# Start of a two-stage kernel: the first angle table, the first transform and the first weights in another order

## Chip, core and metric

The kernel runs on one core of one Trainium2 chip. The metric is the device time of one execution in microseconds, smaller is better. A core has five engines that run their own instruction queues in order: TensorE (PE, matrix products), VectorE (DVE), ScalarE (ACT), GpSimd (POOL) and SyncE (SP). They wait for each other through semaphores. PSUM is where TensorE writes, SBUF is the memory of the core.

## The reference

`x` has 8 batches of 3008 rows by 256 columns. The first stage is the real part of a two-dimensional Fourier transform of each batch, the second a feed-forward layer with a squared ReLU on every row:

```python
def _attn_ref(x) -> np.ndarray:
    X = np.fft.fft(x, axis=1)
    X = np.fft.fft(X, axis=2)
    return X.real.astype(np.float32)

def _moe_ref(x, w_in, w_out) -> np.ndarray:
    h = np.maximum(x @ w_in, 0.0)
    return (h * h @ w_out).astype(np.float32)
```

`w_in` is 256 by 2048, `w_out` 2048 by 256. The result has 24064 rows of 256 columns.

## The kernel before

The rows of a batch are folded first: sums and differences of row n and row S-n, and of column d and column D-d, so that the transform over the rows needs only a part of the products. A folded batch has two units: `(i, 0)` with the odd frequencies and `(i, 1)` with the even ones. For each unit TensorE multiplies folded rows by tables of cosines and sines (`z_steps`, L560; the matmul is L581), and ACT and VectorE bring the result into windows of up to 512 columns, `zc` and `zs` (L586, L592, L599, L610). The transform over the 256 columns is not made for each row: it is multiplied into `w_in` beforehand. `gh_step` (L519) multiplies a block of 512 columns of `w_in` by the cosines `c_all` and the sines `s_n` of the column transform, VectorE scales the result into `gh` (`gh_scale`, L513, here L517), and `gh_turn` (L532) makes a third copy with the sign turned.

The windows then run one after the other: `gh` times `zc` and `zs` (L859, L860, L868, L877, L882; L938 and L944 in the first window), ReLU on ACT (L891, L950) or VectorE (L889), square on VectorE or ACT, and the product with `w_out` (L704) for the window before, whose rows go out through SP. Folds and transforms of later batches are spread over the steps of the windows. The order on every engine is the order in which the program writes the instructions; no scheduler changes it.

All that the change touches is written ahead of the first window:

- POOL issues the loads of the first `x` (a direct transfer of the first two quarters, then one gathered transfer for the third and one for the fourth, L127 and L132), with small index tables in between, then the two halves of `w_in` (L180). Later it issues the load of `w_out` (L329).
- `table_steps(0)` (L207) makes the table for unit 0: 128 partitions, 6 rows, 376 frequencies. Rows stand in the order `RQ = (1, 3, 5, 0, 2, 4)`; set 0 is rows 1, 3, 5, set 1 is rows 0, 2, 4. `freq` (L220) makes the frequencies `kf` on VectorE from `irow`, a cast of the integers `irow_i`. `args` (L227) makes three rows of rounded turns on ACT, `turns` (L236) turns them into multiples of the length on VectorE or POOL. The angle, `kf` times the row number plus that multiple, is made in one of two ways: by `mods` (L250), a multiply-add on VectorE for each row, or by `kns` (L240), the products on ACT, and `sums` (L246), one addition over three rows on VectorE. Before, set 0 goes by `mods` and set 1 by `kns` and `sums`.
- `sins` (L259) takes the sine of three rows on ACT. `weigh` (L273) multiplies row 1 of the sines by a weight `wgt`, on POOL. A cosine row is the mirrored sine row 6-r, so `coss` (L262) is a matmul with a mirroring matrix `perm` (made on POOL, L326) and an eviction on ACT (L271), two rows at a time: rows 1 and 3, rows 5 and 0, rows 2 and 4.
- `c_all` and `s_n` are made from 129 columns of `irow` on VectorE (L289 to L301) and by two sines on ACT (L315, L317), with one column of `s_n` copied from `c_all` (L331).
- `fold_steps(0)` (L372) folds the first batch: `u_half` (L395) subtracts the first two quarters and copies one row of `x`, `u_odd` (L399) subtracts the other two, `u_part(sg)` (L402) makes `cs` and folds the columns into `od[:, sg]`, `edge` (L406) copies one column of it on ACT, `nyq` (L450) fills another by two small matmuls and a VectorE copy (L455), `v_even` (L409) makes the other half of the fold and issues the load of the next batch.
- `idle(n)` (L304) puts n matmuls on TensorE whose result nobody reads.
- `z0(part, h)` is the first transform: part 0 with cosines, part 1 with sines, h is the set. After h 0 ACT copies the sum out of PSUM (`es`), and the second half adds to the same PSUM tile.

PSUM tiles come from three pools: `ps_h` (2 tiles of two banks), `ps_o` (2 tiles of one bank, tag `po`) and `ps_z` (2). A new tile of a pool waits until the one two before it has been read.

The order of the start before, from L309 on:

```python
    run(f0s["u_half"], f0s["u_odd"], lambda: f0s["u_part"](0))
    to["coss"](0)
    idle(4)
    to["coss"](1)
    to["coss"](2)
    idle(5)
    f0s["edge"]()
    run(*z0(0, 0))
    gh_pg = gh_step(0)
    run(lambda: f0s["u_part"](1), f0s["nyq"])
    gh_scale(gh[:, 0:2, 0:512], gh_pg, False)
    run(*z0(0, 1))
    run(*z0(1, 0))
    gh_turn(0)
    gh_step(1, False)
```

Of the kernel before, what the change touches and what calls it, by code (L numbers as in the profile page):

```python
# [29 lines left out]
def kernel(  # L30
# [152 lines left out]
    def small(shape, name):  # L183
        return const.tile(shape, F32, name=name)
# [7 lines left out]
    nraw = small([P, R], "nraw")  # L192
    nc.vector.tensor_copy(nraw, nvec_i)
    irow = small([P, NE], "irow")
    nc.vector.tensor_copy(irow, irow_i)
# [11 lines left out]
    def table_steps(e):  # L207
# [12 lines left out]
        def freq():  # L220
            kf = st["kf"] = tmp.tile([P, NE], F32, name="kf", tag="kf")[:, 0:n]
            i = 0
            for k0, kstep, cnt in unit_runs[e][0]:
                nc.vector.tensor_scalar(out=kf[:, i : i + cnt], in0=irow[:, i : i + cnt], scalar1=float(kstep), scalar2=float(k0 - kstep * i), op0=ALU.mult, op1=ALU.add)
                i += cnt

        def args(h):  # L227
# [19 lines left out]
            m = st["m", h][:, 0:nr, 0:n]  # L247
            nc.vector.tensor_tensor(m, m, st["t", h][:, 0:nr, 0:n], op=ALU.add)

        def mods(h):  # L250
            m = st["m", h] = tmp.tile([P, 3, NE], F32, name="m", tag="tm")
            for j in range(nr):
                r = row(h, j)
                nc.vector.scalar_tensor_tensor(out=m[:, j, 0:n], in0=st["kf"], scalar=vec[:, r : r + 1], in1=st["t", h][:, j, 0:n], op0=ALU.mult, op1=ALU.add)

        def absm(h):
            nc.vector.tensor_scalar(out=st["t", h][:, 0:nr, 0:n].bitcast(I32), in0=st["m", h][:, 0:nr, 0:n].bitcast(I32), scalar1=0x7FFFFFFF, scalar2=None, op0=ALU.bitwise_and)

        def sins(h):  # L259
            nc.scalar.activation(sin_t[:, 3 * h : 3 * h + nr, :], st["m", h][:, 0:nr, 0:n], AF.Sin, bias=0.0, scale=wk)  # L260

        def coss(h):  # L262
            if e:
                nc.scalar.activation(cos_t, st["t", h][:, 0:nr, 0:n], AF.Sin, bias=halfpi[:, 0:1], scale=-wk)
                return

            pc = ps_h.tile([P, 2, 512], F32, name="pc", tag="psh")
            for j in range(2):
                r = RQ[2 * h + j]
                nc.tensor.matmul(pc[:, j, 0:n], perm[1 if r else 0], sin_t[:, RQ.index(6 - r if r else 0), :], start=True, stop=True)  # L270
            nc.scalar.activation(cos_t[:, 2 * h : 2 * h + 2, :], pc[:, :, 0:n], AF.Copy, bias=0.0, scale=1.0)  # L271

        def weigh():  # L273
            if e:
                for t in (cos_t, sin_t):
                    for r in range(2):
                        nc.vector.tensor_scalar(out=t[:, r, :], in0=t[:, r, :], scalar1=wge[:, r : r + 1], scalar2=None, op0=ALU.mult)
                return

            q = RQ.index(1)  # L280
            nc.gpsimd.tensor_scalar(out=sin_t[:, q, :], in0=sin_t[:, q, :], scalar1=wgt[:, 0:1], scalar2=1.0, op0=ALU.mult, op1=ALU.mult)
# [22 lines left out]
    def idle(n):  # L304

        for i in range(n):
            nc.tensor.matmul(pw[:, 0 : 3 * P], spn[:, 0, 0, :], spn.rearrange("p c r d -> p (c r d)")[:, 0 : 3 * P], start=True, stop=True)
# [7 lines left out]
    nc.scalar.activation(s_n, am, AF.Sin, bias=0.0, scale=-wd)  # L315
    c_all = const.tile([P, 2, P + 1], F16, name="c_all")
    nc.scalar.activation(c_all, at, AF.Sin, bias=halfpi[:, 0:1], scale=-wd)  # L317
# [6 lines left out]
    perm = [const.tile([P, P], F16, name=f"perm{i}") for i in range(2)]  # L324
    for i in (1, 0):
        nc.gpsimd.tensor_scalar(out=perm[i], in0=prow_i, scalar1=float(P - 1 - i), scalar2=None, op0=ALU.is_equal)  # L326
    to["sums"](1)

    nc.gpsimd.dma_start(out=wout16, in_=moe_w_out.rearrange("(c p) o -> p c o", p=P))  # L329
# [3 lines left out]
    pick = const.tile([P, 1], F16, name="pick")  # L333
    nc.gpsimd.memset(pick, 0.0)
# [4 lines left out]
    evec_i = iota([P, 2], [[1, 2]], 0, 2, "evec_i")
    idx["c"] = iota([P, 1], [[1, 1]], P - 1, -1, "idx_c")  # L340
    nc.gpsimd.memset(idx["c"][0:2, :], P - 3)
    idx["f"] = iota([P, 1], [[1, 1]], -1, 1, "idx_f")
    nc.gpsimd.memset(idx["f"][0:1, :], 0)
    evec = small([P, 2], "evec")
    nc.gpsimd.tensor_copy(evec, evec_i)
    evs = small([P, 2], "evs")
    nc.gpsimd.tensor_scalar(out=evs, in0=evec, scalar1=1.0 / S, scalar2=None, op0=ALU.mult)
    wge = small([P, 2], "wge")
    wg2 = small([P, 2], "wg2")
    nc.gpsimd.tensor_scalar(out=wge, in0=evec, scalar1=float(G), scalar2=0.5, op0=ALU.is_le, op1=ALU.mult)  # L350
    nc.gpsimd.tensor_scalar(out=wg2, in0=evec, scalar1=float(G), scalar2=0.5, op0=ALU.is_lt, op1=ALU.mult)
    nc.gpsimd.tensor_tensor(wge, wge, wg2, op=ALU.add)
    nc.gpsimd.tensor_scalar(out=wg2, in0=evec, scalar1=0.0, scalar2=-0.5, op0=ALU.is_equal, op1=ALU.mult)
    nc.gpsimd.tensor_tensor(wge, wge, wg2, op=ALU.add)
    to["sins"](1)
    folded = {}

    fe = fo = None
# [13 lines left out]
    def fold_steps(i):  # L372
# [21 lines left out]

        def u_half():  # L395
            nc.vector.tensor_tensor(u[:, 0], t[:, 0], t[:, 1], op=ALU.subtract)
            nc.vector.tensor_copy(t[0:1, 2, 0, :], t[0:1, 0, R - 1, :])

        def u_odd():  # L399
# [109 lines left out]
        return {"edge": edge, "u_half": u_half, "u_odd": u_odd, "u_part": u_part, "v_even": v_even, "v_part": v_part, "d_even": d_even, "n_cos": n_cos, "odds": odds, "d_odd": d_odd, "load": load, "n_sin": n_sin, "nyq": nyq, "even": even, "away": away, "back": back, "late": late}  # L509

    gh = const.tile([P, 3, F], F16, name="gh")

    def gh_scale(out, pg, act):  # L513
        if act:
            nc.scalar.activation(out, pg, AF.Copy, bias=0.0, scale=-1.0 / HS)
        else:
            nc.vector.tensor_scalar(out=out, in0=pg, scalar1=-1.0 / HS, scalar2=None, op0=ALU.mult)  # L517

    def gh_step(cc, act=None):  # L519

        f0 = cc * 512
        fw = f0 % (F // 2)
        pg = ps_h.tile([P, 2, 512], F32, name="pg", tag="psh") if act is None else None
        for i, t in enumerate((c_all, s_n)):
            pt = ps_o.tile([P, 512], F32, name="pg", tag="po") if pg is None else pg[:, i, :]
            for c in range(2):
                nc.tensor.matmul(pt, t[:, c, 0:P], w16[f0 // (F // 2)][:, c, fw : fw + 512], start=(c == 0), stop=(c == 1))
# [535 lines left out]
```

## Time and profile before

| | |
|---|---|
| median of three runs | 598.36 us (597.36 to 598.58) |
| the profiled execution | 597.31 us |
| its span, first to last instruction | 595.5 us |
| mean granted TensorE clock | 0.999 |
| instructions | 11299 |

The profile is one execution. Busy time is given for PE, PEld (TensorE's weight loads, which overlap PE), DVE, ACT and POOL. A row of the timeline is one instruction, or several of a line merged: its start, its length, engine, line, operation, what it writes and reads, and in brackets how long the engine stood idle before it and what ended that. The chain is followed back from the last instruction to what released each step.

### The profile page before, as it was taken

What the parts mean: (1) busy time and instruction counts of PE and PEld (TensorE: products, weight loads), DVE (VectorE), ACT (ScalarE), POOL (GpSimd) and SP (SyncE); (2) the same over time, 40 slices, a digit from 0 to 9 for tenths busy, and PEclk for the clock granted to TensorE, in tenths of its full rate; (3) what the DMA queues carried; (4) which work ended last, traced back from release to release, by engine and by line L of the source; (5) the groups of instructions that cost most, each with busy time, mean ns of one, the idle gap of its engine ahead of it and who ended that gap; (6) DMA issues with size and microseconds to landing.
All of it is one profiled execution on the core that took longest, in us unless ns stands there. A gap on an engine that the chain in (4) does not pass through costs nothing.

```text
span 595.5 us, 11299 instructions
## 1 busy us (share of the span) xinstructions
PE 584.9 (98%) x4421; PEld 424.9 (71%) x4421; DVE 497.0 (83%) x582; ACT 462.2 (78%) x617; POOL 243.9 (41%) x304
## 2 busy tenths in 40 slices
PE   7999999999999999999999999999999999999997
PEld 4567786776776777777777777777777777777786
DVE  8988686987989778979899799979899799888871
ACT  6796777967797787788878788877877788788762
POOL 8411423166514506183253651446505724425310
PEclk9999999999999999999999999999999999999999
DMA  8946421137211461246123442145312321211212
GB/s 149 154 87 149 123 73 44 48 108 148 61 44 55 129 138 49 72 101 155 41 59 108 94 116 58 38 121 115 90 39 90 87 58 37 61 47 48 61 56 70
DMA packets 37624, 50.33 MB, mean 85 GB/s; under 512 B 4589, under 2 KB 30755, under 8 KB 37571
## 3 DMA queue, kind: packets, MB, share of 16 engines
q0 software_dynamic: 10400, 24.94, 20.6%
q1 hardware_dynamic: 26899, 24.44, 13.6%
q8 instruction: 34, 0.56, 0.4%
q10 hardware_dynamic: 272, 0.23, 0.1%
q14 instruction: 19, 0.16, 0.1%
HBM read 36.42 MB, written 27.86 MB: 108 GB/s over the span
## 4 chain that ended last, share of the span: by engine, by line
PE 81%; DVE 10%; ACT 3%; POOL 2%; issue 2%; DMA 1%; DVEq 0%; ACTq 0%; POOLq 0%
PE po L704 47%; PE ph L882 6%; PE ph L859 6%; PE ph L860 6%; PE ph L877 6%; PE ph L868 5%; PE pz L581 4%; DVE h L898 2%; DVE t L872 2%; DVE h L889 2%; DMA xo<-in_x_dram,idx_r 1%; ACT h L891 1%; DVE zc L610 1%; ACT h L902 1%; POOL xo L132 1%
## 5 line engine op out<-in xcount | busy, mean ns | idle before, releaser
L704 PE MATMUL po<-wout,h 128*128 128x256 f16 (+1 forms) x3024 | 364.8, 273 | 0.0
L704 PEld LDWEIGHTS <-h 128*128 128x128 f16 (+1 forms) x3024 | 296.8, 98 | 75.1
L891 ACT ACTIVATE h<-ph 128x1024 f16<-128x1024 f32 (+3 forms) x301 | 287.6, 991 | 64.2 <-PE ph L877 41.1
L898 DVE TENSOR_TENSOR h<-h 128x2048 f16<-128x2048 f16 (+7 forms) x199 | 189.9, 960 | 22.1 <-ACT h L891 18.9
L818 POOL TENSOR_SCALAR n<-zn,g2n 128x512 f32<-128x512 f16 (+3 forms) x166 | 156.2, 954 | 68.7 <-DMA zn<-rd 55.5
L872 DVE SCALAR_TENSOR_TENSOR t<-ph,n 128x1024 f32<-128x1024 f32 (+3 forms) x83 | 99.1, 1194 | 37.5 <-PE ph L868 32.1
L889 DVE CUSTOM_DVE_ANT_0 h<-t,ph 128x1024 f16<-128x1024 f32 x74 | 90.0, 1216 | 15.5 <-ACT h L891 15.1
L902 ACT ACTIVATE h<-h 128x1024 f16<-128x1024 f16 (+3 forms) x87 | 90.3, 1038 | 0.5
L719 ACT ACTIVATE osb<-po 128x512 f32<-128x512 f32 (+3 forms) x95 | 55.0, 584 | 37.0 <-PE po L704 32.5
L859 PE MATMUL ph<-zc,gh 128*128 128x512 f16 (+3 forms) x218 | 80.3, 369 | 0.4 <-ACT h L950 0.3
L860 PE MATMUL ph<-zs,gh 128*128 128x512 f16 (+3 forms) x218 | 80.2, 368 | 0.0
L810 POOL DMA_DIRECT2D zn<-rd x22 | 12.7, 579 | 161.9 <-DMA rd<-zs 153.6
L882 PE MATMUL ph<-zs,gh 128*128 128x512 f16 (+3 forms) x218 | 62.5, 368 | 0.3 <-ACT h L891 0.3
L877 PE MATMUL ph<-zs,gh 128*128 128x512 f16 (+3 forms) x166 | 48.4, 373 | 0.9 <-DVE t L872 0.4
L868 PE MATMUL ph<-zc,gh 128*128 128x512 f16 (+3 forms) x166 | 48.4, 373 | 0.0
L859 PEld LDWEIGHTS <-gh 128*128 128x128 f16 x218 | 21.2, 97 | 22.9 <-DVE h L889 1.6
L860 PEld LDWEIGHTS <-gh 128*128 128x128 f16 x218 | 21.3, 98 | 22.1 <-issue 0.9
L868 PEld LDWEIGHTS <-gh 128*128 128x128 f16 x166 | 16.2, 98 | 18.9 <-issue 0.5
L882 PEld LDWEIGHTS <-gh 128*128 128x128 f16 x218 | 20.2, 98 | 4.1 <-issue 0.7
L586 ACT ACTIVATE es<-pz 128x376 f32<-128x376 f32 (+1 forms) x32 | 14.8, 485 | 8.9 <-PE pz L581 8.7
L464 POOL DMA_DIRECT2D scr<-ev x8 | 4.7, 582 | 40.7 <-DVE ev L460 34.8
L132 POOL DMA_INDIRECT xo<-in_x_dram,idx_r x15 | 17.7, 1182 | 4.5 <-issue 4.3
(143 smaller groups left out, 368.2 us busy)
## 6 DMA issues: line engine op xcount, KB each, us to landing
out_dram<-osb SPq DMA_DIRECT2D x77, 128.0 KB
xo<-in_x_dram POOLq DMA_DIRECT2D x7, 768.0 KB, 6.8
scr<-ev POOLq DMA_DIRECT2D x8, 390.0 KB, 4.0
zn<-rd POOLq DMA_DIRECT2D x19, 128.0 KB, 3.9
rb<-scr POOLq DMA_DIRECT2D x16, 130.0 KB, 3.9
out_dram<-osb SPq DMA_DIRECT2D x12, 94.0 KB
w<-in_moe_w_in_dram POOLq DMA_DIRECT2D x2, 512.0 KB, 10.0
wout<-in_moe_w_out_dram POOLq DMA_DIRECT2D x1, 1024.0 KB, 11.0
```

The costliest lines, as they stand in the source:

```text
L704: nc.tensor.matmul(po[0:m, j * D : (j + 1) * D], h2[:, fc, q : q + m], wout16[:, fc, :], start=(fc == 0 and not both), stop=(fc == NFC - 1 ...
L818: nc.gpsimd.tensor_scalar(out=n2[:, a, 0:wn1], in0=zns[wt][:, 0:wn1], scalar1=g2n[:, fc : fc + 1], scalar2=1.0, op0=ALU.mult, op1=ALU.mult)
L859: nc.tensor.matmul(ph[:, a, 0:wn], gh[:, 0, f0 : f0 + P], zcw[:, 0:wn], start=True, stop=False)
L860: nc.tensor.matmul(ph[:, a, 0:wn], gh[:, 1, f0 : f0 + P], zsw[:, 0:wn], start=False, stop=True)
L868: nc.tensor.matmul(ph[:, a, 0:wn], gh[:, 0, f0 : f0 + P], zcw[:, 0:wn], start=True, stop=True)
L872: nc.vector.scalar_tensor_tensor(out=t2[:, :, 0:wn], in0=phs[s][:, :, 0:wn], scalar=-2.0, in1=n2s[w, s][:, :, 0:wn], op0=ALU.mult, op1=ALU ...
L877: nc.tensor.matmul(phs[s][:, a, 0:wn], gh[:, 1, f0 : f0 + P], zsw[:, 0:wn], start=False, stop=True, skip_group_check=True)
L882: nc.tensor.matmul(phs[s][:, a, 0:wn], gh[:, 2, f0 : f0 + P], zsw[:, 0:wn], start=False, stop=True, skip_group_check=True)
L889: nc.vector._custom_dve(TENSOR_ADD_SAT, out=h, in0=t2s[s][:, :, 0:wn], in1=phs[s][:, :, 0:wn], s0=BIG, s1=0.0)
L891: nc.scalar.activation(h, phs[s][:, :, 0:wn], AF.Relu, bias=0.0, scale=-1.0)
L898: nc.vector.tensor_tensor(h, h, h, op=ALU.mult)
L902: nc.scalar.activation(h, h, AF.Square, bias=0.0, scale=1.0)
```

## The change

`freq` of set `table_steps(0)` reads the integers `irow_i` directly, and the cast to `irow` moves behind it. Set 0 of the angles is made by `kns` and `sums`, set 1 by `mods` in two calls, two rows and one row. The sines of set 1 are taken in two calls as well. `weigh` moves from POOL to ACT, and the two instructions for `wgt` from POOL to VectorE. `coss` has four parts instead of three (rows 1 and 3, row 5, row 0, rows 2 and 4), its matmuls and its eviction can be written apart, and its one-row parts take their PSUM tile from `ps_o`. The row copy of `u_half` becomes a step of its own, `u_row`. `s_n` and `c_all` come after the first three cosine rows on ACT. Fillers are 48 and 14 instead of 44, 4 and 5. The small POOL setup from `pick` to `wge` comes after the second set of sines, the `w_out` load directly after the second `perm`. In the first transform the last three cosine rows come after `gh_step(0)`, and `gh_step(1)`, `gh_turn(0)`, `z0(1, 0)` come ahead of `z0(0, 1)`. The functions of `fold_steps` to `z_steps` are defined earlier in the file, otherwise unchanged.

```diff
     irow = small([P, NE], "irow")
-    nc.vector.tensor_copy(irow, irow_i)
...
-                nc.vector.tensor_scalar(out=kf[:, i : i + cnt], in0=irow[:, i : i + cnt], scalar1=float(kstep), scalar2=float(k0 - kstep * i), op0=ALU.mult, op1=ALU.add)
+                nc.vector.tensor_scalar(out=kf[:, i : i + cnt], in0=(irow if e else irow_i)[:, i : i + cnt], scalar1=float(kstep), scalar2=float(k0 - kstep * i), op0=ALU.mult, op1=ALU.add)
...
-        def mods(h):
-            m = st["m", h] = tmp.tile([P, 3, NE], F32, name="m", tag="tm")
-            for j in range(nr):
+        def mods(h, js=None):
+            if not js or 0 in js:
+                st["m", h] = tmp.tile([P, 3, NE], F32, name="m", tag="tm")
+            m = st["m", h]
+            for j in js or range(nr):
...
-        def sins(h):
-            nc.scalar.activation(sin_t[:, 3 * h : 3 * h + nr, :], st["m", h][:, 0:nr, 0:n], AF.Sin, bias=0.0, scale=wk)
+        def sins(h, a=0, z=nr):
+            nc.scalar.activation(sin_t[:, 3 * h + a : 3 * h + z, :], st["m", h][:, a:z, 0:n], AF.Sin, bias=0.0, scale=wk)
...
-            pc = ps_h.tile([P, 2, 512], F32, name="pc", tag="psh")
-            for j in range(2):
-                r = RQ[2 * h + j]
+            q0, nq = ((0, 2), (2, 1), (3, 1), (4, 2))[h]
+            pc = ps_h.tile([P, 2, 512], F32, name="pc", tag="psh") if nq > 1 else ps_o.tile([P, 512], F32, name="pc", tag="po").rearrange("p (j n) -> p j n", j=1)
+            for j in range(nq):
+                r = RQ[q0 + j]
...
-            nc.scalar.activation(cos_t[:, 2 * h : 2 * h + 2, :], pc[:, :, 0:n], AF.Copy, bias=0.0, scale=1.0)
+            return lambda: nc.scalar.activation(cos_t[:, q0 : q0 + nq, :], pc[:, :, 0:n], AF.Copy, bias=0.0, scale=1.0)
...
-            nc.gpsimd.tensor_scalar(out=sin_t[:, q, :], in0=sin_t[:, q, :], scalar1=wgt[:, 0:1], scalar2=1.0, op0=ALU.mult, op1=ALU.mult)
+            nc.scalar.activation(sin_t[:, q, :], sin_t[:, q, :], AF.Copy, bias=0.0, scale=wgt)
...
     to["freq"]()
+    nc.vector.tensor_copy(irow, irow_i)
...
-    idle(44)
-    to["args"](0)
-    to["args"](1)
-    to["kns"](1)
-    nc.scalar.activation(s_n, am, AF.Sin, bias=0.0, scale=-wd)
-    nc.scalar.activation(c_all, at, AF.Sin, bias=halfpi[:, 0:1], scale=-wd)
-    to["turns"](0)
-    to["mods"](0)
-    to["turns"](1, nc.gpsimd)
-    nc.gpsimd.tensor_scalar(out=wgt, in0=nraw[:, 1:2], scalar1=float(Q), scalar2=-0.5, op0=ALU.is_equal, op1=ALU.mult)
-    nc.gpsimd.tensor_scalar(out=wgt, in0=wgt, scalar1=1.0, scalar2=None, op0=ALU.add)
-    for i in (1, 0):
-        nc.gpsimd.tensor_scalar(out=perm[i], in0=prow_i, scalar1=float(P - 1 - i), scalar2=None, op0=ALU.is_equal)
-    to["sums"](1)
-    nc.gpsimd.dma_start(out=wout16, in_=moe_w_out.rearrange("(c p) o -> p c o", p=P))
-    to["sins"](0)
-    nc.scalar.activation(s_n[:, :, 0:1], c_all[:, :, P : P + 1], AF.Copy, bias=0.0, scale=0.5)
-    to["weigh"]()
...
-    to["sins"](1)
...
-    run(f0s["u_half"], f0s["u_odd"], lambda: f0s["u_part"](0))
-    to["coss"](0)
-    idle(4)
-    to["coss"](1)
-    to["coss"](2)
-    idle(5)
+    def make_perm(i):
+        nc.gpsimd.tensor_scalar(out=perm[i], in0=prow_i, scalar1=float(P - 1 - i), scalar2=None, op0=ALU.is_equal)
+
+    idle(48)
+    to["args"](0)
+    to["kns"](0)
+    to["args"](1)
+    make_perm(1)
+    to["turns"](0)
+    to["sums"](0)
+    to["turns"](1, nc.gpsimd)
+    make_perm(0)
+    nc.gpsimd.dma_start(out=wout16, in_=moe_w_out.rearrange("(c p) o -> p c o", p=P))
+    to["sins"](0)
+    nc.vector.tensor_scalar(out=wgt, in0=nraw[:, 1:2], scalar1=float(Q), scalar2=-0.5, op0=ALU.is_equal, op1=ALU.mult)
+    nc.vector.tensor_scalar(out=wgt, in0=wgt, scalar1=1.0, scalar2=None, op0=ALU.add)
+    to["weigh"]()
+    f0s["u_half"]()
+    to["mods"](1, (0, 1))
+    run(f0s["u_row"], f0s["u_odd"], lambda: f0s["u_part"](0))
+    to["mods"](1, (2,))
+    for c in (to["coss"](0), to["coss"](1)):
+        c()
+    idle(14)
+    nc.scalar.activation(s_n, am, AF.Sin, bias=0.0, scale=-wd)
+    nc.scalar.activation(c_all, at, AF.Sin, bias=halfpi[:, 0:1], scale=-wd)
+    nc.scalar.activation(s_n[:, :, 0:1], c_all[:, :, P : P + 1], AF.Copy, bias=0.0, scale=0.5)
+    to["sins"](1, 0, 2)
     f0s["edge"]()
+    to["sins"](1, 2, 3)
...
     run(*z0(0, 0))
     gh_pg = gh_step(0)
+    for c in (to["coss"](2), to["coss"](3)):
+        c()
     run(lambda: f0s["u_part"](1), f0s["nyq"])
     gh_scale(gh[:, 0:2, 0:512], gh_pg, False)
-    run(*z0(0, 1))
-    run(*z0(1, 0))
-    gh_turn(0)
-    gh_step(1, False)
+    gh_step(1, False)
+    gh_turn(0)
+    run(*z0(1, 0))
+    run(*z0(0, 1))
     rm = z0(0, 2) + z0(1, 2)
```

More of the change, by code (lines that the diff above doesn't have):

```diff
@@ L307, in idle @@
             nc.tensor.matmul(pw[:, 0 : 3 * P], spn[:, 0, 0, :], spn.rearrange("p c r d -> p (c r d)")[:, 0 : 3 * P], start=True, stop=True)
-    idle(44)
-    to["args"](0)
-    to["args"](1)
-    to["kns"](1)
+    perm = [const.tile([P, P], F16, name=f"perm{i}") for i in range(2)]
     wd = 2.0 * math.pi / D
     s_n = const.tile([P, 2, P + 1], F16, name="s_n")
-    nc.scalar.activation(s_n, am, AF.Sin, bias=0.0, scale=-wd)
     c_all = const.tile([P, 2, P + 1], F16, name="c_all")
-    nc.scalar.activation(c_all, at, AF.Sin, bias=halfpi[:, 0:1], scale=-wd)
@@ L339 @@
[L339 to L354, printed above, removed]
-    to["sins"](1)
     folded = {}
@@ L396, in u_half, with u_row @@
             nc.vector.tensor_tensor(u[:, 0], t[:, 0], t[:, 1], op=ALU.subtract)
+        def u_row():
             nc.vector.tensor_copy(t[0:1, 2, 0, :], t[0:1, 0, R - 1, :])
@@ L508, in fold_steps @@
         late = [lambda: fold8(0), lambda: fold8(1), lambda: fold16(0), lambda: fold16(1), nyq8]
-        return {"edge": edge, "u_half": u_half, "u_odd": u_odd, "u_part": u_part, "v_even": v_even, "v_part": v_part, "d_even": d_even, "n_cos": n_cos, "odds": odds, "d_odd": d_odd, "load": load, "n_sin": n_sin, "nyq": nyq, "even": even, "away": away, "back": back, "late": late}
+        return {"u_row": u_row, "edge": edge, "u_half": u_half, "u_odd": u_odd, "u_part": u_part, "v_even": v_even, "v_part": v_part, "d_even": d_even, "n_cos": n_cos, "odds": odds, "d_odd": d_odd, "load": load, "n_sin": n_sin, "nyq": nyq, "even": even, "away": away, "back": back, "late": late}
     gh = const.tile([P, 3, F], F16, name="gh")
@@ new lines @@
+    for c in (to["coss"](0), to["coss"](1)):
[5 more added lines that the diff above has]
+    to["sins"](1, 0, 2)
+    f0s["edge"]()
+    to["sins"](1, 2, 3)
+    pick = const.tile([P, 1], F16, name="pick")
+    nc.gpsimd.memset(pick, 0.0)
+    nc.gpsimd.memset(pick[0:1, :], -2.0)
@@ new lines @@
+    turn2 = small([P, 1], "turn2")
+    nc.gpsimd.tensor_scalar(out=turn2, in0=dvec[:, 0:1], scalar1=0.0, scalar2=2.0, op0=ALU.is_equal, op1=ALU.mult)
+    nc.gpsimd.tensor_scalar(out=turn2, in0=turn2, scalar1=-2.0, scalar2=None, op0=ALU.add)
+    evec_i = iota([P, 2], [[1, 2]], 0, 2, "evec_i")
+    idx["c"] = iota([P, 1], [[1, 1]], P - 1, -1, "idx_c")
+    nc.gpsimd.memset(idx["c"][0:2, :], P - 3)
+    idx["f"] = iota([P, 1], [[1, 1]], -1, 1, "idx_f")
+    nc.gpsimd.memset(idx["f"][0:1, :], 0)
@@ new lines @@
+    evec = small([P, 2], "evec")
+    nc.gpsimd.tensor_copy(evec, evec_i)
+    evs = small([P, 2], "evs")
+    nc.gpsimd.tensor_scalar(out=evs, in0=evec, scalar1=1.0 / S, scalar2=None, op0=ALU.mult)
+    wge = small([P, 2], "wge")
+    wg2 = small([P, 2], "wg2")
+    nc.gpsimd.tensor_scalar(out=wge, in0=evec, scalar1=float(G), scalar2=0.5, op0=ALU.is_le, op1=ALU.mult)
+    nc.gpsimd.tensor_scalar(out=wg2, in0=evec, scalar1=float(G), scalar2=0.5, op0=ALU.is_lt, op1=ALU.mult)
+    nc.gpsimd.tensor_tensor(wge, wge, wg2, op=ALU.add)
@@ L653 @@
+    nc.gpsimd.tensor_scalar(out=wg2, in0=evec, scalar1=0.0, scalar2=-0.5, op0=ALU.is_equal, op1=ALU.mult)
+    nc.gpsimd.tensor_tensor(wge, wge, wg2, op=ALU.add)
     run(*z0(0, 0))
     gh_pg = gh_step(0)
+    for c in (to["coss"](2), to["coss"](3)):
+        c()
     run(lambda: f0s["u_part"](1), f0s["nyq"])
     gh_scale(gh[:, 0:2, 0:512], gh_pg, False)
+    gh_step(1, False)
+    gh_turn(0)
+    run(*z0(1, 0))
     run(*z0(0, 1))
-    run(*z0(1, 0))
-    gh_turn(0)
-    gh_step(1, False)
     rm = z0(0, 2) + z0(1, 2)
```

7 lines of the change are left out of this document (removed).

## The prediction

> **What bounds the kernel now.** I read the page's busy times and its chain first, then the timeline of the first 50 us engine by engine, since the change ends there. Columns of the timeline: start and length in us, engine, line, operation, and in brackets the idle time before it with what ended it.
>
> ```profile
> PE 584.9 (98%) x4421; PEld 424.9 (71%) x4421; DVE 497.0 (83%) x582; ACT 462.2 (78%) x617; POOL 243.9 (41%) x304
> PE 81%; DVE 10%; ACT 3%; POOL 2%; issue 2%; DMA 1%; DVEq 0%; ACTq 0%; POOLq 0%
> ```
>
> TensorE is busy nearly throughout and is 81% of the chain, so work saved on another engine is worth only what it brings TensorE's queue forward. TensorE's opening:
>
> ```profile
> 1.22 10.05 PE L307 MATMUL pw<-spn 128*128 128x384 f16 x44 [1.22 <-DVE spn L189]
> 6.63 4.24 PEld L307 LDWEIGHTS <-spn 128*128 128x128 f16 x26 [0.17 <-issue]
> 14.44 0.80 PE L270 MATMUL pc<-sin,perm 128*128 128x376 f16 x4 [2.00 <-POOL pick L334]
> 16.62 0.65 PE L581 MATMUL pz<-cos,od 128*128 128x376 f16 x3 [0.56 <-ACT od L407]
> 18.98 0.59 PE L527 MATMUL pg<-w,c_all 128*128 128x512 f16 x2
> 19.84 0.64 PE L581 MATMUL pz<-sin,od 128*128 128x376 f16 x3
> 20.94 0.57 PE L938 MATMUL ph<-zs,gh 128*128 128x240 f16 x4
> 23.86 0.59 PE L527 MATMUL pg<-w,c_all 128*128 128x512 f16 x2
> 24.46 0.59 PE L527 MATMUL pg<-w,s_n 128*128 128x512 f16 x2
> 44.10 0.65 PE L581 MATMUL pz<-sin,od 128*128 128x376 f16 x3 [0.46 <-DVE od L455]
> ```
>
> The first 44 matmuls are filler. The first useful transform, z0(0,0), starts at 16.62, held by ACT's edge copy (L407). Before it TensorE stood still for 2.00 us: the view names the POOL instruction after it, but the matmul's wait is on `weigh` (L281), which ends at 14.39 below. ACT:
>
> ```profile
> 4.04 3.10 ACT L232 ACTIVATE t<-kf,nvs 128x376 f32<-128x376 f32 x6 [1.81 <-DVE kf L224]
> 7.05 1.59 ACT L244 ACTIVATE m<-kf,nvec 128x376 f32<-128x376 f32 x3
> 8.54 0.40 ACT L315 ACTIVATE s_n<-am 128x258 f16<-128x258 f32 x1
> 8.85 0.50 ACT L317 ACTIVATE c_all<-at,halfpi 128x258 f16<-128x258 f32 x1
> 10.12 1.14 ACT L260 ACTIVATE sin<-m 128x1128 f16<-128x1128 f32 x1 [0.77 <-DVE m L254]
> 14.96 1.49 ACT L271 ACTIVATE cos<-pc 128x752 f16<-128x752 f32 x2 [1.74 <-PE pc L270]
> 16.33 0.23 ACT L407 ACTIVATE od<-cs 128x6 f16<-128x6 f16 x1
> 17.31 0.48 ACT L586 ACTIVATE es<-pz 128x376 f32<-128x376 f32 x1 [0.74 <-PE pz L581]
> ```
>
> **First angles: args, kns, turns, sums.** VectorE and POOL:
>
> ```profile
> 2.91 0.36 DVE L195 CAST irow<-irow_i 128x377 f32<-128x377 int32 x1
> 3.66 0.35 DVE L224 TENSOR_SCALAR kf<-irow 128x376 f32<-128x376 f32 x1
> 6.32 1.07 DVE L238 TENSOR_SCALAR t<-t 128x1128 f32<-128x1128 f32 x1
> 9.94 1.41 DVE L248 TENSOR_TENSOR m<-m,t 128x1128 f32<-128x1128 f32 x1
> ...
> 7.44 1.14 POOL L238 TENSOR_SCALAR t<-t 128x1128 f32<-128x1128 f32 x1
> 9.66 2.09 POOL L326 TENSOR_SCALAR perm<-prow_i 128x128 f16<-128x128 int32 x2
> 11.71 1.23 POOL L329 DMA_DIRECT2D wout<-in_moe_w_out_dram  x1
> 13.03 1.36 POOL L281 TENSOR_SCALAR sin<-sin,wgt 128x376 f16<-128x376 f16 x1
> ```
>
> The cast of irow leaves the path to kf: kf can come at most 0.36 earlier; I take 0.25 (ACT starts at 3.80), as the casts overlap their neighbours. Nine ACT instructions go from 4.04 to 8.54, 0.50 each. With the order args(0), kns(0), args(1), kns(0) is done at 6.9 and args(1) at 8.4. turns(0) still ends at 7.39, because the am/at work before it on VectorE keeps its length (the cast only moves behind kf). Then sums(0), at its own 1.41, runs 7.45 to 8.87, where the three L254 ran until 10.02. So sins(0) runs 8.97 to 10.11 instead of 10.12 to 11.26: 1.15 us earlier. `weigh` on ACT is one more 376-column instruction: between 0.48 (L586) and 0.60 (L232); with 0.60 it ends at 10.75 instead of 14.39 on POOL.
>
> **Filler and cosines.** 48 fillers instead of 44: 26 weight loads take 4.24 us, 0.16 each, so four more cost 0.65 and TensorE reaches the first cosine matmuls at 11.75, not when the sines are ready. This eats 1 us of the gain above, and it is cover too: a delay of the sines up to 1 us costs nothing. Three matmuls 0.16 apart, the first two done at 12.23; from there ACT's queue sets the path: cosines of rows 1 and 3 at 12.27 (0.70 start to start, half of 1.49 rounded down for overlap), row 5 (0.39, half the columns), s_n (0.31, from 8.54 to 8.85), c_all and its one-column fix (0.63), sins(1) of two rows (0.74, two thirds of 1.14), edge (0.23). Sum 3.00: edge ends at 15.27 and z0(0,0) can start at 15.32, against 16.62: 1.30 us earlier, if VectorE's od is there.
>
> **VectorE around u.**
>
> ```profile
> L254 DVE SCALAR_TENSOR_TENSOR m<-kf,nvec,t x3: 598/600/1551, 7.4 to 9.4; 128x376 f32<-128x376 f32 x3
> 11.28 1.04 DVE L396 TENSOR_TENSOR u<-xo 128x1536 f16<-128x1536 f16 x1
> 12.24 0.71 DVE L397 COPY xo<-xo 1x256 f16<-1x256 f16 x1
> 12.99 0.96 DVE L400 TENSOR_TENSOR u<-xo 128x1536 f16<-128x1536 f16 x1
> 13.98 1.22 DVE L403 TENSOR_TENSOR cs<-u 128x1536 f16<-128x1536 f16 x1
> 15.23 0.57 DVE L370 TENSOR_TENSOR od<-cs 128x768 f16<-128x768 f16 x1
> 18.20 0.18 DVE L455 CAST od<-py 128x6 f16<-128x6 f32 x1 [0.95 <-PE py L454]
> 21.46 1.75 DVE L410 TENSOR_TENSOR v<-xo 128x3072 f16<-128x3072 f16 x1
> ...
> L400 DVEq EVENT_SEMAPHORE  x1: 21/21/21, 12.1 to 12.1; - x1
> ```
>
> The last row is u_odd's wait for the last quarter of x, over at 12.1: u_odd can't start sooner, so at most 0.9 of its 12.99 is to be had. Two things may keep it later. One L254 took 1551 ns instead of 600 beside POOL's turns(1) (7.44 to 8.58), and L397 ended at 12.95 just as POOL's issue of wout ended at 12.94: VectorE waits out long POOL instructions. Now turns(1) starts on POOL when args(1) or sums(0) ends, so it runs to between 9.6 and 10.0, and u_half stands behind it to between 10.4 and 11.0. Two mods of 0.52 follow, and the row copy waits out the wout issue again, which ends between 11.7 and 12.6 as one perm goes ahead of turns(1). Bounds of u_odd: 12.1 and 12.95; I take 12.5. cs at 13.5 costs 0.96 like L400, not 1.22, because `weigh` no longer runs on POOL beside it. od is done at 15.05, inside ACT's 15.32 (15.5 at the late bound). The third mods (0.60), cs and od of the other part end at 17.07, against 17.26.
>
> A rule on the same rows: the Trainium skill, SBUF — State Buffer, section Who interferes with whom, says that a VectorE instruction with two SBUF inputs and a GpSimd one that reads SBUF exclude each other for the whole instruction, whichever starts first. The 1551 ns agree; the two perms beside L248 agree less: it took 1.41 for 1128 columns, where three undisturbed L254 take 1.57 for as many. What the rule in full would make of the time is the slow rival below.
>
> **TensorE from z0(0,0).** From 16.62 to 20.94 it took 4.32 before. Moved in between are the three late cosine matmuls: 0.48. gh_step(1) now takes its PSUM buffer after the row-0 cosine, so it waits for ACT's eviction (matmul done at 16.99, 0.48 long, 17.50): TensorE, ready at 17.20, loses 0.35. z0(1,1) follows z0(0,1) directly, where gh_step(1) (18.98 to 19.84) covered the es eviction before: es ends at 19.57, TensorE is ready at 19.36, loses 0.26 with the latency. ACT's sins of the third row (ready for it at 15.67) end at 16.17, before TensorE needs them at 16.83: slack 0.66. In sum quad's second half comes at 20.72 instead of 20.94: of 1.30 only 0.22 is left.
>
> VectorE keeps more: its copy L455 comes at 17.39 instead of 18.20, since the 0.95 wait goes, and the six instructions from there to v_even take 3.26 before, some 3.1 in the new order: v_even at 20.5 instead of 21.46. The next load of x is issued behind it and everything on VectorE up to 43.9 is 1 us earlier. That removes the 0.17 that TensorE lost between 23.86 and 24.46 (0.60 where 0.43 is usual, waiting for VectorE's evictions), so the gain is 0.39 there; and at 44.10 the 0.46 wait for L455 shrinks to copy and latency: 0.55 in all. POOL's small setup (pick to wge) only slides along, wout lands long before its first use. After 44.10 the order is unchanged and TensorE carries the gain to the end.
>
> Sum: 597.31 of the profiled execution (span 595.5 and 1.8 around it) less 0.55 is 596.76. That execution lies 1.05 under the median of the runs, 598.36; at their level it is 597.8.
>
> **The rivals.**
> Fast: ACT's queue between 15.3 and 19.6 is looser than I add up, and the two new stalls (0.35 and 0.26) vanish, with od at its early bound. For it: ACT had 0.74 idle before es and has no POOL neighbour. Against: two of its instructions wait for matmuls that are fixed by TensorE's own order. Time: 0.55 plus 0.61 plus up to 0.2, 1.3 in all: 597.1.
>
> Hidden: VectorE's 1 us is lost in front of v_even, or the next x does not land earlier, so L455 near 43.87 still decides. For it: TensorE's 0.46 wait at 44.10 was VectorE's. Against: nothing new stands in that queue. Time: 598.36, no gain.
>
> Slow: POOL and VectorE exclude each other for whole instructions, in POOL's worst order. sums(0) first, to 8.8; perm (0.78, the shorter of the 2.09) to 9.6; turns(1) 1.14 to 10.8; u_half 0.96 to 11.76; the other perm to 12.55; two mods to 13.65, with the wout issue beside them to 13.85; then the row copy and u_odd at 14.1. It decides from u_odd at 13.4 on, where the 0.66 slack and the 0.22 are used up roughly together. At 14.1 od is done at 16.65 and z0(0,0) starts at 16.7, 1.4 later than forecast: 0.55 of gain becomes 0.85 to 1.2 of loss, 599.2 to 599.6. Against it: L248 beside the perms. The page named above is the rule that gives this.
>
> **How the numbers follow.** Forecast 0.41, fast 0.34, hidden 0.07, slow 0.18. Within 0.2%, 1.2 us, is about what a measurement of this kernel can tell from no change. Forecast and hidden fall inside it, with a few hundredths of the forecast over the fast edge; the fast rival at 1.3 is mostly outside; of the slow one most, if sums, u and cosines all slip together. So faster 0.36, same 0.48, slower 0.16. The range goes from the fast rival with both bounds added (1.8) less half the runs' own spread (0.6), 596.0, to the slow one, 599.6; the forecast's own is 597.2 to 598.4.
>
> **What would show it.** sins(0) ending near 10.1 and first cosine matmul near 11.75 (filler, not data, sets it); u_odd between 12.1 and 12.95; z0(0,0) near 15.3 released by the edge copy; a stall in front of gh_step(1) and of z0(1,1); v_even near 20.5; the transform now at 44.10 near 43.5. Wrong if u_odd starts after 13.4, if the filler ends with another clock, or if z0(0,0) moves and quad's second half keeps the whole 1.3.

## The result and the profile after

| | before | after |
|---|---|---|
| median of 20 executions each, side by side | 598.32 us (597.23 to 598.93) | 596.77 us (596.57 to 597.15) |
| the profiled execution | 597.31 us | 596.79 us |
| its span | 595.5 us | 595.0 us |

The ratio after to before is 0.9979, 95% interval 0.9973 to 0.9985: faster by 0.21%. In the means that is 1.25 us (598.05 to 596.80); the medians lie 1.55 us apart. The two profiled executions differ by 0.52 us only. Where the rest comes from is the question of the experiments.

The busy times and the chain of the page of after:

```profile
PE 586.2 (99%) x4430; PEld 426.0 (72%) x4430; DVE 499.4 (84%) x584; ACT 463.0 (78%) x620; POOL 242.2 (41%) x301
PE 85%; DVE 7%; ACT 5%; issue 2%; ACTq 0%; DVEq 0%
```

POOL and DMA, 2% and 1% of the chain before, no longer stand in it. The timeline of TensorE in after; columns are start and length in us, engine, line, operation, and in brackets the idle time ahead with what ended it:

```profile
11.81 0.64 PE L272 MATMUL pc<-sin,perm 128*128 128x376 f16 x3
...
15.33 0.65 PE L543 MATMUL pz<-cos,od 128*128 128x376 f16 x3 [0.61 <-ACT od L369]
...
17.58 0.59 PE L489 MATMUL pg<-w,c_all 128*128 128x512 f16 x2 [0.22 <-ACT cos L273]
...
18.92 0.64 PE L543 MATMUL pz<-cos,od 128*128 128x376 f16 x3
19.65 0.64 PE L543 MATMUL pz<-sin,od 128*128 128x376 f16 x3
...
20.75 0.57 PE L947 MATMUL ph<-zs,gh 128*128 128x240 f16 x4
...
23.66 0.59 PE L489 MATMUL pg<-w,c_all 128*128 128x512 f16 x2
24.09 0.59 PE L489 MATMUL pg<-w,s_n 128*128 128x512 f16 x2
...
43.56 0.65 PE L543 MATMUL pz<-sin,od 128*128 128x376 f16 x3 [0.29 <-DVE od L417]
```

The reader sees the first transform at 15.33 instead of 16.62, released by the edge copy (L369 here). Of these 1.29 us, 0.19 are left at the second half of the first quad, the sine half (`zs`) of the first products with `gh` (L938 before, L947 here; 20.75 against 20.94): the three cosine matmuls now stand in between, and there are two stalls, one ahead of gh_step(1) (17.58), one ahead of z0(1,1) (19.65). From VectorE more is left: 24.09 follows 23.66 at the usual 0.43, and the transform that came at 44.10 comes at 43.56.

VectorE of after, its start:

```profile
7.71 1.33 DVE L247 TENSOR_TENSOR m<-m,t 128x1128 f32<-128x1128 f32 x1
...
9.21 1.63 DVE L356 TENSOR_TENSOR u<-xo 128x1536 f16<-128x1536 f16 x1
10.77 1.15 DVE L255 SCALAR_TENSOR_TENSOR m<-kf,nvec,t 128x376 f32<-128x376 f32 x2
11.84 0.58 DVE L359 COPY xo<-xo 1x256 f16<-1x256 f16 x1
12.45 0.96 DVE L362 TENSOR_TENSOR u<-xo 128x1536 f16<-128x1536 f16 x1
13.45 0.96 DVE L365 TENSOR_TENSOR cs<-u 128x1536 f16<-128x1536 f16 x1
14.44 0.57 DVE L330 TENSOR_TENSOR od<-cs 128x768 f16<-128x768 f16 x1
```

And POOL of after beside it:

```profile
8.51 1.53 POOL L237 TENSOR_SCALAR t<-t 128x1128 f32<-128x1128 f32 x1 [0.48 <-ACT t L231]
10.12 1.11 POOL L607 TENSOR_SCALAR perm<-prow_i 128x128 f16<-128x128 int32 x1
11.18 1.23 POOL L620 DMA_DIRECT2D wout<-in_moe_w_out_dram  x1
```

The first half of u (L356) takes 1.63 us, 0.59 more than before's 1.04, while POOL's turns(1) runs to 10.04. The row copy (L359) takes 0.58 and ends with POOL's issue, 12.42 against 12.41. ACT of after shows the two steps that free the path, the sines and the weighting of their row 1:

```profile
9.08 1.14 ACT L261 ACTIVATE sin<-m 128x1128 f16<-128x1128 f32 x1 [0.65 <-DVE m L247]
10.25 0.61 ACT L283 ACTIVATE sin<-sin,wgt 128x376 f16<-128x376 f16 x1
...
15.07 0.21 ACT L369 ACTIVATE od<-cs 128x6 f16<-128x6 f16 x1
```

### The profile page after: what moved, and what is told of

Its sections match the earlier page's. It is cut to its first block, busy times and chain, and to the rows that moved or that the text cites. A ratio compares the mean times of both kernels' runs of the same rounds, so it can differ in the third digit from the quotient of the medians.

```text
span 595.0 us, 11318 instructions
## 1 busy us (share of the span) xinstructions
PE 586.2 (99%) x4430; PEld 426.0 (72%) x4430; DVE 499.4 (84%) x584; ACT 463.0 (78%) x620; POOL 242.2 (41%) x301
## 3 DMA queue, kind: packets, MB, share of 16 engines
q0 software_dynamic: 10400, 24.94, 20.5%
## 4 chain that ended last, share of the span: by engine, by line
PE 85%; DVE 7%; ACT 5%; issue 2%; ACTq 0%; DVEq 0%
PE po L713 48%; PE ph L891 7%; PE ph L868 7%; PE ph L869 7%; PE ph L886 6%; PE ph L877 5%; PE pz L543 4%; DVE h L907 2%; ACT h L900 2%; PE pw L310 2%; DVE t L881 2%; DVE h L898 2%; ACT h L911 1%; PE pg L489 1%; DVE zc L572 1%
## 5 line engine op out<-in xcount | busy, mean ns | idle before, releaser
L907 DVE TENSOR_TENSOR h<-h 128x2048 f16<-128x2048 f16 (+7 forms) x199 | 193.2, 977 | 21.9 <-ACT h L900 16.9
L436 POOL DMA_INDIRECT rb<-scr,idx_r x16 | 18.7, 1167 | 4.9 <-issue 4.9
```

The source lines that it names most:

```text
L907: nc.vector.tensor_tensor(h, h, h, op=ALU.mult)
```

## The experiments

Before's times fall into two groups with nothing between: of 84 executions 39 lie at 597.17 to 597.80 (median 597.45) and 45 at 598.11 to 598.93 (median 598.44). After's 20 lie in one. My theory: TensorE's standstill of 2.00 us ahead of 14.44 makes the granted clock drop behind it in part of before's executions, and the change fills that standstill. Its rivals put the second group on POOL and VectorE or on the transfers, or hold that the reordering itself is the gain.

**Before once more.** The kernel before, unchanged, to profile an execution of each group.

> The kernel before, unchanged, looked at again. Its 20 times lie in two groups, 8 from 597.23 to 597.65 and 12 from 598.27 to 598.93; the profiled one, 597.31, is of the lower. In the changed kernel all 20 lie between 596.57 and 597.15. Theory 1 (clock): a profile of the upper group has about 1 us more on TensorE because the granted clock falls to one half behind the 2.0 us standstill at 12.4 to 14.4, so matmuls of the same size take twice as long for 1 to 3 us somewhere between 12 and 20 us. Theory 2 (turn of VectorE and POOL): the clock is whole everywhere, and weigh on POOL (1.36 us, 13.03 to 14.39) ends about 1 us later because another VectorE instruction goes ahead of it. Theory 3 (transfer): the last quarter of x lands 1 us later than 12.06. If the profile is of the lower group it shows none of the three and spans 595.5 again.

> The same kernel before once more, for a second draw between the two groups: 12 of 20 executions were in the upper one. The same three readings as for b1; if both fall into the upper group, they must show the same mark in the same place.

> The kernel before, a third look, for a profile of its upper group (about 55 of 100 executions; b1 and b2 were of the lower). e_pool's profile showed the granted clock at one half for 3.4 us behind a standstill of TensorE of 3.0 us. Clock theory: an execution above 598 shows the same here, matmuls 0.32 apart for one stretch of about 3.4 us that begins within 1 to 4 us of the standstill's end at 14.4, and spans 596.5 to 597. If it falls into the lower group again it shows nothing new.

The 20 times beside after split nine to eleven, not eight to twelve as the first two texts say. The standstill that the third text gives as 3.0 us, in a run shown further down, is 2.66 in its trace. The first two runs gave 597.68 and 597.42 us, both in the lower group, and show nothing new at the start. The third gave 598.66. TensorE in this third profile of before:

```profile
14.43 0.80 PE L270 MATMUL pc<-sin,perm 128*128 128x376 f16 x4 [2.00 <-POOL pick L334]
...
16.60 1.12 PE L581 MATMUL pz<-cos,od 128*128 128x376 f16 x3 [0.38 <-ACT od L407]
17.52 1.06 PE L527 MATMUL pg<-w,c_all 128*128 128x512 f16 x2
18.37 0.98 PE L527 MATMUL pg<-w,s_n 128*128 128x512 f16 x2
...
22.16 0.57 PE L938 MATMUL ph<-zs,gh 128*128 128x240 f16 x4
```

z0(0,0) starts when it always did, but three matmuls take 1.12 instead of 0.65 and two take 1.06 instead of 0.59; the quad's second half is 1.22 late. POOL's weighting (13.02) and VectorE's u_odd (12.97) start there within 0.02 of the first profile (13.03 and 12.99), so neither POOL and VectorE nor the transfer that u_odd waits for came late. The windows of the same profile, and then of the first profile of before (a row has the stretch, its length, the busy time of the engines in turn, the granted clock, the DMA share and the GB/s):

```profile
14.43:15.72 1.29, 1.29 (x9) 0.78 (x8) 1.26 (x3) 0.77 (x2) 1.16 (x3) 1.00 1.11 210
15.72:19.13 3.41, 3.03 (x9) 1.04 (x8) 1.49 (x3) 1.31 (x4) 2.51 (x13) 0.50 1.33 198
19.13:21.00 1.87, 1.87 (x13) 0.99 (x12) 1.47 (x3) 0.97 (x3) 0.00 (x0) 1.00 1.46 199
```

```profile
15.72:19.13 3.41, 2.85 (x19) 1.40 (x17) 2.43 (x5) 1.70 (x5) 2.52 (x13) 1.00 1.32 199
```

For 3.41 us the clock is at half; in the lower group it is whole. The mean granted clock of every execution says the same without a profile: in the 64 executions of before that ran beside the experiments, all 34 above 598 us have 0.995 to 0.997, all 30 below have 0.998 to 1.000. So the clock makes the two groups; whether the standstill makes the clock drop is for the next runs.

**Fill the standstill and change nothing else.**

```diff
-    idle(4)
+    idle(16)
```

> The kernel before with 16 fillers instead of 4 after the first cosine matmuls, which keeps TensorE busy through the 2.0 us in which it waits for weigh (12 more at 0.16 are 1.95 us) and changes no other engine. By theory 1 (clock) the upper group of times disappears: all near 597.5, median 0.9 under the kernel before. By theories 2 and 3 both groups stay, 8 to 12, and the median is that of before within 0.2.

597.40 us (597.28 to 597.56, 11 executions), ratio 0.9991 [0.9982, 1.0]; mean clock 0.999 or 1.000 in all of them. Before's two groups have medians of 597.58 and 598.40 in the same session. TensorE of it:

```profile
14.45 0.80 PE L270 MATMUL pc<-sin,perm 128*128 128x376 f16 x4
...
16.62 0.65 PE L581 MATMUL pz<-cos,od 128*128 128x376 f16 x3 [0.56 <-ACT od L407]
```

The upper group is gone, and nothing else moved: the same work starts at the same time. POOL, VectorE and the transfers are as before, so they don't make the group.

**Lengthen the standstill.**

```diff
-    idle(4)
```

> The kernel before without the 4 fillers between the first cosine matmuls and the wait for weigh, so TensorE stands still from 11.8 to 14.4 instead of 12.4 to 14.4; nothing waits for the fillers. Clock theory: now more executions, perhaps all, fall into the upper group: median 598.4 or more, and a profile of such an execution shows matmuls of 376 columns 0.32 apart instead of 0.16 in some stretch behind the standstill, worth about 1 us. Rival (the upper group has nothing to do with TensorE's standstill, and e_fill's 11 quiet runs were luck or a shift of something else): the two groups stay 45 to 55, times unchanged.

598.21 us (597.51 to 598.70, 10 executions), ratio 1.0003 [0.9994, 1.0013]. Of ten, eight have a mean clock of 0.996 or 0.997 (597.82 to 598.70) and two have 1.000 (597.51 and 597.60). The profiled one was one of the two, so no drop is seen in its trace, though its standstill is 2.65 us. Eight of ten against 34 of 64 points to more drops behind a longer standstill, but ten are too few to show it; that not every execution drops is plain.

**Open the hole in after.**

```diff
-    idle(14)
```

> The changed kernel without its 14 fillers behind the first cosine matmuls, so that TensorE stands still from 12.3 to 15.3 with nothing else changed; no instruction waits for these fillers. Clock theory: the two groups come back; some executions near 596.8 as before, others 0.8 to 2 us above, median 597.5 or more. Rival: the changed kernel is quiet because of its other parts (angles, order of POOL), and the fillers are worth nothing: all near 596.8.

597.97 us (596.57 to 598.13, 11 executions), ratio to before 0.9996 [0.9987, 1.0006]. Two executions, at 596.57 and 596.67, keep the clock (0.999); nine, at 597.80 to 598.13, lose it (0.996 or 0.997). TensorE and one window of its profile:

```profile
15.13 0.78 PE L543 MATMUL pz<-cos,od 128*128 128x376 f16 x3 [3.49 <-DVE od L330]
15.70 1.06 PE L489 MATMUL pg<-w,c_all 128*128 128x512 f16 x2
```

```profile
15.50:18.91 3.41, 3.41 (x13) 1.40 (x12) 1.71 (x4) 1.70 (x4) 2.25 (x7) 0.50 1.30 200
```

The same 3.41 us at half clock, in the kernel that had lost them. Without its 14 fillers the change is no longer to be told from before.

**The weighting on ACT alone, in the kernel before.**

```diff
-            nc.gpsimd.tensor_scalar(out=sin_t[:, q, :], in0=sin_t[:, q, :], scalar1=wgt[:, 0:1], scalar2=1.0, op0=ALU.mult, op1=ALU.mult)
+            nc.scalar.activation(sin_t[:, q, :], sin_t[:, q, :], AF.Copy, bias=0.0, scale=wgt)
```

> The kernel before with one part of the change alone: weigh on ACT instead of POOL. My theory of the result: the 2.00 us standstill of TensorE was the wait for weigh, so this alone moves z0(0,0) from 16.62 to 15.5 (ACT: sins(1) ends at 13.1, cosines 13.1 to 15.1, edge behind them), and since the first transform keeps its old order it keeps the whole 1.1 us: span 594.4, against 595.0 of the changed kernel, which gave back 1.1 of its 1.3 between z0(0,0) and the first window. Rival: the reordering of the transform and of the weights is what carries the gain, and weigh alone gives 0.2 or less (span 595.3). By theory 1 of b1 the upper group also goes, as the standstill shrinks to about 1 us: median near 596.2. By theory 2 it goes too; by theory 3 it stays.

596.43 us (596.35 to 596.52, 8 executions), ratio 0.9973 [0.9962, 0.9983]; mean clock 0.999 or 1.000 throughout. One line does more than the whole change: it lies 1.15 below the lower group of before in its own session (597.58), after lies 0.71 below that of its session (597.48). TensorE of it:

```profile
11.31 0.48 PE L270 MATMUL pc<-sin,perm 128*128 128x376 f16 x2 [0.23 <-ACT sin L260]
...
13.05 0.32 PE L270 MATMUL pc<-sin,perm 128*128 128x376 f16 x1 [0.45 <-ACT sin L260]
13.73 0.48 PE L270 MATMUL pc<-sin,perm 128*128 128x376 f16 x2 [0.36 <-ACT cos L271]
...
15.69 0.64 PE L581 MATMUL pz<-cos,od 128*128 128x376 f16 x3 [0.67 <-DVE od L370]
...
20.00 0.57 PE L938 MATMUL ph<-zs,gh 128*128 128x240 f16 x4
```

In place of the 2.00 us there are pauses of at most 0.67 us. z0(0,0) starts 0.36 later than in after, and yet the quad's second half comes 0.75 earlier: from the one to the other it takes 4.31, as before (4.32), and after takes 5.42. At the transform of the next unit 0.35 of the 0.75 is left (43.21 against 43.56), which is what the times show.

**The rest of the change without it.**

```diff
-            nc.scalar.activation(sin_t[:, q, :], sin_t[:, q, :], AF.Copy, bias=0.0, scale=wgt)
+            nc.gpsimd.tensor_scalar(out=sin_t[:, q, :], in0=sin_t[:, q, :], scalar1=wgt[:, 0:1], scalar2=1.0, op0=ALU.mult, op1=ALU.mult)
```

> The changed kernel with weigh back on POOL, all else as changed. My theory: the rest of the change alone is a loss. POOL comes to weigh only behind the issue of w_out, at 12.4, and shares with u_odd there, so it ends at 13.0 to 13.8; the cosine of row 5 is evicted at 13.5 to 14.3 and everything behind it on ACT (s_n, c_all, sins, edge) slides by 0.5 to 1.2: z0(0,0) at 15.8 to 16.5, span 595.5 to 596.3, and the standstill of TensorE comes back in another place. Rival: the other parts (angles by sums, early sines, split cosines) carry the gain: span 595.0 as changed.

598.39 us (597.29 to 599.53, 11 executions), ratio 1.0008 [0.9999, 1.0018]. Four executions, 599.45 to 599.53, have a clock of 0.997, the profiled one among them; seven have 0.999 or 1.000, one at 597.29 and six at 598.05 to 598.59. TensorE of the profiled one:

```profile
10.78 0.48 PE L272 MATMUL pc<-sin,perm 128*128 128x376 f16 x2
13.91 0.32 PE L272 MATMUL pc<-sin,perm 128*128 128x376 f16 x1 [2.66 <-POOL pick L639]
14.07 3.72 PE L310 MATMUL pw<-spn 128*128 128x384 f16 x14
17.59 1.07 PE L543 MATMUL pz<-cos,od 128*128 128x376 f16 x3
```

Row 1 waits for the weighting again (the view names the instruction behind it), the 14 fillers behind it run at half clock (3.72 us) and hold up z0(0,0), whose last input, the edge copy, was ready at 16.53. So fillers can also harm: they stand in TensorE's queue ahead of the useful work. Leaving the weighting on POOL takes the whole gain away.

**The order behind gh_step(0).**

```diff
-    gh_step(1, False)
-    gh_turn(0)
-    run(*z0(1, 0))
+    run(*z0(1, 0))
+    gh_step(1, False)
+    gh_turn(0)
     run(*z0(0, 1))
```

> The changed kernel with z0(1,0) ahead of gh_step(1) again, so that gh_step(1) covers the es eviction for z0(1,1); z0(0,1) stays behind gh_step(1). My theory: the 0.26 stall before z0(1,1) goes and the 0.36 stall moves in front of z0(1,0), which then waits for the VectorE copy of nyq (17.59): quad's second half at 20.55 instead of 20.75, span 594.8, 0.2 faster. Rival: TensorE's stalls there are hidden by the ReLUs on ACT in the first window: span 595.0, same.

596.64 us (596.42 to 597.26, 9 executions), ratio 0.9976 [0.9966, 0.9986]. TensorE of it:

```profile
15.47 0.65 PE L543 MATMUL pz<-cos,od 128*128 128x376 f16 x3 [0.61 <-ACT od L369]
...
17.79 0.65 PE L543 MATMUL pz<-sin,od 128*128 128x376 f16 x3 [0.29 <-DVE od L417]
...
20.72 0.57 PE L947 MATMUL ph<-zs,gh 128*128 128x240 f16 x4
```

From z0(0,0) to the quad's second half 5.25 instead of 5.42: one of the two stalls is gone, the other has moved to z0(1,0), which waits for VectorE's copy. That is 0.17 us in the trace. The medians, 0.13 apart, don't decide so little, and the profiled execution was its slowest.

**Six fillers fewer.**

```diff
-    idle(48)
+    idle(42)
```

> The changed kernel with 42 fillers instead of 48 at the start. By the prediction's step that the filler and not the sines sets the first cosine matmul (11.81 measured, sines ready at 10.22, weighed at 10.86), six fillers fewer bring it to 10.85, and ACT's queue then waits for VectorE: edge behind cs (14.40), z0(0,0) behind od (15.01) at 15.06 instead of 15.33. All behind moves with it: span 594.7, 0.27 faster. Rival: the fillers are what keeps the clock whole; with six fewer the times split into two groups, the upper about 1 us slower.

596.64 us (596.57 to 597.11, 9 executions), ratio 0.9977 [0.9967, 0.9987]. TensorE of it:

```profile
10.95 0.64 PE L272 MATMUL pc<-sin,perm 128*128 128x376 f16 x3
...
15.13 0.64 PE L543 MATMUL pz<-cos,od 128*128 128x376 f16 x3 [1.27 <-DVE od L330]
...
20.54 0.57 PE L947 MATMUL ph<-zs,gh 128*128 128x240 f16 x4
```

The first cosines come 0.86 earlier, z0(0,0) only 0.20: now VectorE's od sets it (L330), as the prediction's sum has it (15.05 for od). The standstill of 1.27 costs no clock in nine executions. Again 0.21 in the trace and not decided by the medians.

**Two versions that go on from the one line.** In the first the load of `w_out` is also issued behind `pick` and `turn` on POOL; in the second, beside that, the edge copy stands ahead of the last cosine eviction.

```diff
-    nc.gpsimd.dma_start(out=wout16, in_=moe_w_out.rearrange("(c p) o -> p c o", p=P))
...
+    nc.gpsimd.dma_start(out=wout16, in_=moe_w_out.rearrange("(c p) o -> p c o", p=P))
```

```diff
     to["coss"](1)
+    f0s["edge"]()
     to["coss"](2)
     idle(5)
-    f0s["edge"]()
```

> e_weigh (kernel before, weigh on ACT) with the issue of w_out on POOL behind pick and turn2 instead of ahead of them. In e_weigh the row copy on VectorE ran from 12.25 to 12.96 and ended with that issue, and u_odd started at 12.99. Theory (VectorE's copy waits out POOL's issue): the copy takes 0.2, u_odd starts at 12.55, od is done at 15.1 and z0(0,0) starts at 15.25 instead of 15.69, held by edge: span 594.2, 596.0. w_out then lands at about 23 instead of 22.7, long before 30. Rival (the copy is slow for another reason, or the small POOL instructions hold it as well): u_odd stays at 12.9 and the time at 596.4.

> e_best1 with the edge copy ahead of the eviction of the last two cosine rows on ACT; z0(0,0) doesn't need those. Theory: edge no longer stands behind ACT's evictions, z0(0,0) starts right behind od, at 15.15; 0.1 faster than e_best1, 595.9. If the eviction, now later by 0.2, is late for z0(0,1), the gain is given back there.

596.01 us (595.80 to 596.33, 6 executions), ratio 0.9968 [0.9956, 0.998], and 595.96 us (595.82 to 596.25, 6 executions), ratio 0.9965 [0.9953, 0.9978]. VectorE of the first:

```profile
12.26 0.21 DVE L397 COPY xo<-xo 1x256 f16<-1x256 f16 x1
12.51 0.96 DVE L400 TENSOR_TENSOR u<-xo 128x1536 f16<-128x1536 f16 x1
```

With no issue on POOL beside it, but a small POOL instruction (turn, 11.94 to 12.52), the row copy takes 0.21 instead of 0.71, and u_odd starts 0.48 earlier. z0(0,0) starts at 15.24 and the quad's second half at 19.56; in the second version at 15.19 and 19.49. That last 0.07 is gone by the first transform of the next unit (42.66 in the first, 42.71 in the second), so the two are the same.

## Why the prediction was right, and where not

The profiled execution was forecast 0.55 us earlier and is 0.52 earlier, and the places agree: first cosine matmul at 11.75 (measured 11.81), u_odd at 12.5 (12.45), od done at 15.05 (15.01), z0(0,0) at 15.32 (15.33), quad's second half at 20.72 (20.75), the copy on VectorE at 17.39 (17.41), v_even at 20.5 (20.34), the later transform at 43.55 (43.56). The two new stalls, worked out as 0.35 and 0.26, are 0.36 and 0.26. Part of this agreement is luck. The 11.75 was taken from a profile in which the clock rose at 6.80, and it rose at 6.90 in after's; the same 48 fillers ended up to 1.03 earlier in other runs, where it rose earlier (last section).

The time is another matter. At 596.77 it lies outside the forecast's own range (597.2 to 598.4) and inside the whole one (596.0 to 599.6) only by the room left for the fast rival. The larger chance, 0.48, stood on a change within 0.2%, and 0.36 on faster; the measured 0.21% (0.15 to 0.27) lies on that line.

The step that failed is the last one of the sum, "That execution lies 1.05 under the median of the runs, 598.36; at their level it is 597.8." It carried 1.05 us over as if it belonged to any execution. It was the clock's drop, which over half of before's executions had and the profiled one hadn't. In the runs beside after, the lower group of before has a median of 597.48 (nine executions) and all of before 598.32: after's 596.77 is 0.71 below the first, and the other 0.84 of the 1.55 come from executions with the drop. In the means, 0.68 of 1.25 lie below the lower group and 0.57 come from the drop. The prediction costed the fillers as an obstacle and as cover for late sines, and named another clock only for their own end; it did not ask what the 2.00 us standstill it had quoted did to the clock behind it. The time so came out 1.0 below the forecast, near the fast rival's figure but not by its way: both stalls that the fast rival takes away stand in the trace.

Smaller terms: sums(0) ran 7.71 to 9.04, not 7.45 to 8.87, which was covered by the fillers as the prediction says. turns(1) took 1.53 beside VectorE, not 1.14, and held u_half until 10.84, inside the bounds given (10.4 to 11.0). `cs` took 0.96 with the weighting off POOL, and 1.22 again where it was put back and ran beside it. The slow rival's full exclusion in POOL's worst order did not come: u_odd started at 12.45, not 14.1.

The reordering of the transform was counted right, but its worth was not asked for by itself. The runs answer it: the weighting on ACT alone gives 596.43, the rest alone 598.39, both together 596.77. What is spent between z0(0,0) and the quad, 5.42 against 4.31, is 0.48 of cosine matmuls and 0.62 of stalls, and that is more than the 0.36 by which z0(0,0) starts earlier than with the one line alone.

The page TensorE: Matmul & The Clock Gate of the Trainium skill, Part 1, has the clock fall to half after an idle window of about 3.4 us and rise again after a busy one. The length of the drop, 3.41 us in all three traces that show one, agrees. That the window must be idle throughout does not: 2.00 us were enough in 34 of 64 executions, and TensorE was busy for 1.41 of the 3.41 us that end with the drop in the profile at 598.66.

## What to carry to other kernels

Look at the single times before the profile: where they fall into two groups, the one profiled execution stands for one of them, and the mean granted clock of each execution tells which. A standstill of TensorE costs the wait and, with some chance (from 2.00 us on here), a stretch at half clock behind it, so it is worth filling with idle matmuls that end just before the data come, or better, removing at its cause. In a change of many parts try the smallest part that breaks the wait alone: here the one line was better than the whole.

## What was unexpected in the hardware

- The clock dropped for 3.41 us behind a standstill of 2.00 us (34 of 64 executions), of up to 2.65 us without before's four fillers (8 of 10) and of 3.49 us (9 of 11); it didn't behind one of 1.27 us (0 of 9). In the profile with the weighting put back on POOL the standstill was 2.66 us; 4 of its 11 executions dropped.
- What decides between two executions of one kernel is, as far as the traces tell, where a grid of 3.41 us falls. In all fourteen profiles every step of the clock lies a whole number of 3.41 us behind its first rise, and that rise moves from run to run, between 4.42 and 7.18. In the profile at 598.66 the clock rises at 5.48 and falls at 15.72, three steps later; in the two other traces with a drop it rises at 5.26 and 4.81 and falls at 15.50 and 15.05, three steps later too. In the grid step that ends with the fall TensorE stood still for 2.00, 3.04 and 2.28 us. In the first profile of before a grid line at 13.62 cuts the 2.00 us standstill in two; the steps on either side hold 1.23 and 1.39 us of idle time, and the clock stays. Without the four fillers a line at 12.89 cuts the 2.65 us, the steps hold 1.50 and 1.81, and it stays. In no profile does it stay behind a step with more than 2.00.
- One profile stands on the edge: at 597.68 us the step from 12.43 to 15.84 holds the same 2.00 us of idle time as the one at 598.66, and the clock stays. No run moved the grid on purpose, so this account is read from traces and not tested.
- A count of fillers is no fixed time. The 48 of after let the first cosine matmul start at 11.81, the same 48 at 11.95, 11.00 and 10.78 in the kernels with another order, without the hole's fillers and with the weighting on POOL. The clock's first rise accounts for it: 6.90, and 7.18, 5.26 and 4.81. The fillers are 0.32 apart ahead of it and 0.16 behind it, so a rise 1 us earlier ends them 0.5 earlier: 11.95, 10.99 and 10.77 by this sum.
- In the kernel with the weighting on POOL, the six executions at 598.05 to 598.59 with full clock fit the same late weighting with fillers that aren't slowed: z0(0,0) would start behind the edge copy at about 16.6 instead of 17.59 and run 0.42 shorter, 1.4 less than 599.45 and so about 598.0. This is an estimate; none of the six was profiled. The one at 597.29 stays open.
